# An ELU's tail written as a product, with the PSUM readers put first

## The chip, the cores and the metric

One core of one Trainium2 chip runs the kernel. The metric is the device time of one execution in microseconds (us). Engines by their names in the profile: PE (matmul), PEld (weight load), DVE (vector), ACT (activation), POOL (GpSimd), SP (which issues most of the transfers). Each engine works off its own instructions strictly in order and waits on signals of the others.

## The reference, cut to what matters

Three layers follow each other: a linear attention, a mixture of four ReLU experts, and one wide layer with an ELU between two matrix products. The change lies in the last one:

```
h = x @ w_in                      # x: 2304 x 512, w_in: 512 x 2048
g = where(h > 0, h, exp(min(h, 0)) - 1)
out = g @ w_out                   # w_out: 2048 x 512
```

## The kernel before

The products are made in fp32 quality: each operand is split into a high and a low part, and each product is three matmuls (high by high, high by low, low by high). The ELU layer runs as 12 steps, numbered i = 18 to 29: 4 slices of the hidden width (`s` = 6 to 9) by 3 blocks of tokens (`b`). A step has two halves (`fp` = 0, 1), and a half makes a 2 by 2 block of quarters of h by Strassen's scheme with 7 products, p = 0 to 6, each six matmuls on a 128x384 PSUM bank (L1165).

Four PSUM banks A, B, C, D (tiles `h` and `m`, two of each) turn round: the halves exchange A with C and B with D. In a half, p0 goes to C and p1 to B; p2 adds to B, and DVE makes D from it (L1454); p3 adds to A, which is then quarter A11; p4 adds to B, and DVE makes C from it (L1465, called the C add below), which is quarter A22; p5 adds to D, quarter A21; p6 adds to B, quarter A12. The next half's p1 overwrites the bank of A21 and its p0 that of A11, so a bank must have been read by then.

Each quarter goes through `elu` (96 calls: 12 steps, 2 halves, 4 quarters). Its three ACT steps are issued at once; its DVE steps are put into the list `pend` and issued by `run_pend` behind the next product's work. The ACT order and the DVE order are thus fixed by where the code calls these functions; nothing is rescheduled. The names that rows show: `extra` and one `half` are the two buffers of the variable m, another `half` holds t, and the result g goes to `gt` or `half`. From step 21 on (`fast`), quarters are combined on DVE: S1, S2, S3 behind A21 (L1219 to L1221), S4 behind A12 (L1225). What results is split by `parts`: ACT copies the high part (L1187), POOL subtracts for the low part (L1188).

Between the products stand, by a table of places, the second layer's products of the step before (`turned_product`, L1294, 12 matmuls each), whose two PSUM banks are added into SBUF by DVE (L1303), and pieces of weight preparation for later steps (DVE L763, L768, L769, L774, L775, L809, ACT L752, L800, POOL L801). In steps 18 and 19 the next layer's input is also transposed and stored (ACT L957, L974, DVE L985, POOL L991). 

Of the kernel before, what the change touches and what calls it, by code (L numbers as in the profile page):

```python
# [14 lines left out]
AF = mybir.ActivationFunctionType  # L15
ALU = mybir.AluOpType
# [5 lines left out]
def tile_attention_moe_moe(  # L22
# [13 lines left out]
    nc = tc.nc  # L36
# [490 lines left out]
    def bank(which):  # L527
        pool = ps_h if which == "h" else ps[which]
        return pool.tile([P, ps.get((which, "wide"), 1), 512], F32, tag=which, name=which)
# [5 lines left out]
    t = bank("o")  # L535
# [64 lines left out]
    for i in range(NP_):  # L600
        late = i >= NPAIR
        t = K_START[i - NPAIR] if late else HALF_STEP * i
# [243 lines left out]
    for b in range(NB):  # L846
        need = min(NP_, -(-2 * TB * (b + 1) // S) * NPAIR)
        t = 66 + 36 * b
# [302 lines left out]
    def fast(i):  # L1151
        return 0 <= i < len(STEPS) and SEVEN[STEPS[i][0]]

    def turned(i):
        return 0 <= i < len(STEPS) and STEPS[i][0] >= S_MOE

    def product(i, fp, p, dst):
        s, b = STEPS[i]
        wname, xname, o = PRODUCTS[p]
        t, c = w1s[s, fp][wname]  # L1160
        x = [y.rearrange("p (d n) -> p d n", d=2) for y in ring(len(OPS) * i + p)]
        n = 0
        for dl in range(2):
            for wl, xl_ in ((0, 0), (0, 1), (1, 0)):
                nc.tensor.matmul(  # L1165
                    dst, t[:, wl, c + dl, :], x[xl_][:, dl, :], start=(n == 0 and p < 2), stop=(n == 5),
                    skip_group_check=True,
                )
                n += 1
# [5 lines left out]
            out=gl, in0=h, scalar=0.0, in1=gh.bitcast(F32), op0=ALU.max, op1=ALU.subtract  # L1175
        )

    waiting, pend = [], []
    halves, turns = {}, [0]

    def flush():
# [3 lines left out]
    def parts(key, g):  # L1185
        gh, gl = take(*key)
        nc.scalar.activation(out=gh, in_=g, func=AF.Copy)  # L1187
        nc.gpsimd.tensor_tensor(out=gl, in0=g, in1=gh.bitcast(F32), op=ALU.subtract)  # L1188

    def run_pend():  # L1190
        while pend:
            pend.pop(0)()

    def elu(i, h, fp, name):

        if not halves:
            for tag, n in (("qh", 2), ("ql", 2), ("y", 1)):
                t = tmp.tile([P, n * TB], F32, tag=tag, name="half")
                halves[tag] = [t[:, k * TB : (k + 1) * TB] for k in range(n)]
        n = turns[0] % 2  # L1200
        turns[0] += 1
        m, t = (e_, halves["y"][0])[n], halves["qh"][n]
        nc.scalar.activation(out=m, in_=h, func=AF.Relu, scale=-1.0)
        nc.scalar.activation(out=t, in_=m, func=AF.Tanh, scale=-0.5)
        nc.scalar.activation(out=m, in_=m, func=AF.Exp, scale=-1.0)
        if fast(i) and "s4" not in halves:
            halves["s4"] = tmp.tile([P, TB], F32, tag="ek", name="s4")
        g11, g22, s1, s2 = (gt[:, k] for k in range(4))
        g21, g12 = halves["ql"]
        tt = nc.vector.tensor_tensor  # L1210
        g = dict(A11=g11, A22=g22, A21=g21, A12=g12)[name] if fast(i) else halves["ql"][n]

        def rest():
            nc.vector.scalar_tensor_tensor(out=m, in0=m, scalar=1.0, in1=t, op0=ALU.add, op1=ALU.mult)  # L1214
            nc.vector.scalar_tensor_tensor(out=g, in0=h, scalar=0.0, in1=m, op0=ALU.max, op1=ALU.add)  # L1215
            if not fast(i):
                todo = [((int(name[1]) - 1, 2 * fp + int(name[2]) - 1), g)]
            elif name == "A21":
                tt(out=s1, in0=g21, in1=g22, op=ALU.add)  # L1219
                tt(out=s2, in0=s1, in1=g11, op=ALU.subtract)  # L1220
                tt(out=g21, in0=g21, in1=g11, op=ALU.subtract)  # L1221
                todo = [(("S1", fp), s1), (("S2", fp), s2), (("S3", fp), g21)]
            elif name == "A12":
                s4 = halves["s4"]
                tt(out=s4, in0=g12, in1=s2, op=ALU.subtract)  # L1225
                todo = [(("S4", fp), s4), (("A12", fp), g12)]
            else:
                todo = [((name, fp), g)]
            for key, x in todo:
                waiting.append(lambda key=key, x=x: parts((i, *key), x))  # L1230

        pend.append(rest)

    def chunk(i, c):
# [190 lines left out]
    for i, (s, b) in enumerate(STEPS):  # L1425
        moe, fill = s < S_MOE, {}
        if fast(i - 1):
            one, places = (turned_product, TURNED_PLACES) if turned(i - 1) else (second_product, PLACES)
            fill = {n: (one, i - 1, k) for k, n in enumerate(places)}
        elif turned(i - 1):  # L1430
            fill = {n: (group, i - 1, *g) for g, n in zip(GROUPS, GROUP_PLACES)}
        elif i > 0:
            fill = {n: (chunk, i - 1, c) for c, n in zip(CHUNKS, (1, 3, 5, 8, 10, 12) if moe else (1, 2, 5, 8, 9, 12))}
        hooks = TURNED_HOOKS if turned(i - 1) else MIXED if fast(i - 1) else PLAIN if moe else EARLY
        if i + 1 == len(STEPS):
            hooks = {}
        for fp in range(2):
            A_, B_, C_, D_ = (A, B, C, D) if fp == 0 else (C, D, A, B)
            banks = {"A": A_, "B": B_, "C": C_, "D": D_}
            f1, f2 = 2 * fp, 2 * fp + 1  # L1440
            for p in range(len(PRODUCTS)):
                idx = 7 * fp + p
                goal[0] = i * SH + hooks[idx] if idx in hooks else hook2_n[0]
                product(i, fp, p, banks[PRODUCTS[p][2]])
                seven = fast(i)
                if p == 0:
                    nc.scalar.activation(out=s5, in_=C_, func=AF.Copy)
                    run_pend()
                elif p == 1:
                    nc.scalar.activation(out=A_, in_=B_, func=AF.Copy)  # L1450
                    flush_late()
                    flush()
                elif p == 2:
                    nc.vector.tensor_tensor(out=D_, in0=B_, in1=s5, op=ALU.add)  # L1454
                elif p == 3:
                    if moe and seven:
                        quarter_a11(i, fp, A_)
                    elif moe:
                        relu(i, A_, f1, 0)
                    else:  # L1460
                        elu(i, A_, fp, "A11")
                        if idx in fill:
                            run_pend()
                elif p == 4:
                    nc.vector.tensor_tensor(out=C_, in0=B_, in1=s5, op=ALU.add)  # L1465
                    if moe and seven:
                        direct(i, "A22", fp, C_)
                    elif not moe:
                        run_pend()
                        elu(i, C_, fp, "A22")  # L1470
                        flush()
                elif p == 5:
                    if moe and seven:
                        late.extend(quarter_a21(i, fp, D_))
                    elif not moe:
                        run_pend()
                        elu(i, D_, fp, "A21")
                        flush()
                elif p == 6:
                    if idx in fill and moe and fast(i - 1):  # L1480
                        fn, *args = fill.pop(idx)
                        fn(*args)
                    if seven and moe:
                        last = quarter_a12(i, fp, B_)
                        flush_late()
                        late.append(last)
                    elif moe:
                        relu(i, B_, f2, 0)
                    else:
                        run_pend()  # L1490
                        elu(i, B_, fp, "A12")
                        if not seven:
                            flush()
                drain()
                flush_adds()
                if fp == 1:
                    if p == 0:
                        ring_load(len(OPS) * (i + 1))
                    if p < 6:
                        ring_load(len(OPS) * (i + 1) + p + 1)  # L1500
                for _ in range({1: 2, 3: 1, 5: 1, 8: 2, 10: 2}.get(idx, 0) if i == 0 else 0):
                    pieces.pop(0)()
                if idx in fill:
                    fn, *args = fill.pop(idx)
                    fn(*args)
                tick(True)
                if p == 5 and moe and not seven:
                    relu(i, D_, f1, 1)
                    relu(i, C_, f2, 1)
# [59 lines left out]
```

## Time and profile before

| what | value |
|---|---|
| median of 3 runs | 1201.7 us (1200.88 to 1202.17) |
| span of the profiled execution | 1201.4 us |
| granted TensorE clock, mean | 0.994 |
| busy over the span: PE, DVE, ACT, POOL | 97%, 75%, 56%, 53% |
| the ELU layer, from about 808 us to the end | 394 us |

The profiled execution's own time is its span; the median of the runs is 0.3 us above it. PE's busy time is modelled from the starts of pipelined matmuls, so its stalls are read from the idle time ahead of single matmuls, and DVE's and ACT's idle times from theirs. The stretch that counts is the ELU layer, and in it the places where PE stands still.

### The profile page before, as it was taken

How to read it: one execution, taken by the hardware profiler on the slowest of the kernel's cores; microseconds unless marked ns; L12 is line 12 of the kernel's file. 1: busy time of each engine (PE TensorE's matmuls, PEld its weight loads, DVE VectorE, ACT ScalarE, POOL GpSimd, SP SyncE). 2: the span in 40 equal slices, each digit the busy share in tenths (PEclk: the TensorE clock that was granted, in tenths of full speed). 3: DMA queues.
4: the chain of work that ended last, by engine and by line, in shares of the span. 5: the costliest groups of instructions: out<-in, count | busy, mean ns of one | idle time of the engine just before them, and what ended most of it. 6: DMA issues, size and time to landing. Idle time of an engine off the chain costs nothing.

```text
span 1201.4 us, 21064 instructions
## 1 busy us (share of the span) xinstructions
PE 1170.6 (97%) x7516; PEld 1115.4 (93%) x7516; DVE 903.5 (75%) x1525; ACT 673.7 (56%) x1430; POOL 636.7 (53%) x602
## 2 busy tenths in 40 slices
PE   7799999999999999999999999999999999999998
PEld 6688889889999999999999999998999999899898
DVE  6977887655787787787787786566566879879875
ACT  6544544335455455455455453357777777777763
POOL 4622543017468468468468463356535756756744
PEclk7999999999999999999999999999999999999999
DMA  9444666766666666766767767998985465465362
GB/s 254 125 128 154 209 223 212 251 225 220 249 233 245 252 231 245 254 229 246 254 229 245 255 228 264 318 346 268 328 303 203 170 223 176 175 235 184 139 236 105
DMA packets 157399, 272.34 MB, mean 227 GB/s; under 512 B 12784, under 2 KB 83952, under 8 KB 157296
## 3 DMA queue, kind: packets, MB, share of 16 engines
q1 hardware_dynamic: 155568, 267.87, 64.8%
q10 hardware_dynamic: 1728, 3.15, 0.7%
q8 instruction: 59, 0.97, 0.3%
q14 instruction: 44, 0.36, 0.1%
HBM read 224.83 MB, written 46.14 MB: 226 GB/s over the span
## 4 chain that ended last, share of the span: by engine, by line
PE 75%; DVE 12%; ACT 5%; DMA 3%; issue 3%; POOL 2%; SPq 0%; DVEq 0%; POOLq 0%; ACTq 0%
PE o L1383 19%; PE h L1165 14%; PE m L1165 14%; PE h L1021 7%; PE o L1021 7%; PE o L1294 5%; DVE accs L1303 1%; PE o L1249 1%; PE o L1248 1%; PE o L1247 1%; PE o L1269 1%; PE o L1268 1%; PE o L1267 1%; DVE half L1215 1%; DVE extra L1214 1%
## 5 line engine op out<-in xcount | busy, mean ns | idle before, releaser
L1165 PE MATMUL m<-xh,w1s 128*128 128x384 f32 x840 | 246.5, 338 | 5.9 <-DVE half L1215 3.2
L1165 PE MATMUL h<-xh,w1s 128*128 128x384 f32 x840 | 244.9, 337 | 2.6 <-ACT m L1450 1.5
L1165 PEld LDWEIGHTS m<-xh,w1s 128*128 128x128 f32 x840 | 154.2, 188 | 12.0 <-DVE half L1215 4.1
L1165 PEld LDWEIGHTS h<-xh,w1s 128*128 128x128 f32 x840 | 154.8, 188 | 6.1 <-ACT m L1450 2.6
L1165 PE MATMUL m<-xl,w1s 128*128 128x384 f32 x420 | 140.7, 335 | 0.2 <-DMA xl<-xs 0.2
L1165 PE MATMUL h<-xl,w1s 128*128 128x384 f32 x420 | 140.8, 335 | 0.0
L1021 PE MATMUL o<-w2t,hpa 128*128 128x512 f32 x432 | 118.0, 400 | 0.8 <-DVE hpa L1053 0.5
L1021 PE MATMUL h<-xh,w1t 128*128 128x256 f32 (+1 forms) x512 | 112.4, 298 | 0.1
L1021 PEld LDWEIGHTS h<-xh,w1t 128*128 128x128 f32 x512 | 86.4, 193 | 5.2 <-POOL w1t L442 0.3
L1383 PE MATMUL o<-w2g,xh 128*128 128x256 f32 x540 | 90.4, 282 | 0.0
L801 POOL TENSOR_TENSOR w2g<-r,w2g 128x512 fp32r<-128x512 f32 x56 | 77.1, 1385 | 24.0 <-ACT w2g L800 20.2
L1021 PEld LDWEIGHTS o<-w2t,hpa 128*128 128x128 f32 x432 | 75.5, 189 | 14.9 <-DVE hpa L1053 2.4
L1383 PE MATMUL o<-w2g,hpa 128*128 128x256 f32 x540 | 89.0, 282 | 0.0
L1383 PE MATMUL o<-w2g,xl 128*128 128x256 f32 x540 | 87.3, 282 | 0.0
L1405 DVE SCALAR_TENSOR_TENSOR accs<-o,pn,accs 128x256 f32<-128x256 f32 x180 | 75.7, 476 | 14.8 <-PE o L1383 14.2
L1165 PEld LDWEIGHTS m<-xl,w1s 128*128 128x128 f32 x420 | 78.9, 188 | 1.1 <-DMA xl<-xs 0.5
L1165 PEld LDWEIGHTS h<-xl,w1s 128*128 128x128 f32 x420 | 79.2, 189 | 0.3
L1383 PEld LDWEIGHTS o<-w2g,xh 128*128 128x128 f32 x540 | 78.0, 190 | 0.1
L1021 PE MATMUL h<-xl,w1t 128*128 128x256 f32 (+1 forms) x256 | 77.6, 303 | 0.0
L1383 PEld LDWEIGHTS o<-w2g,hpa 128*128 128x128 f32 x540 | 76.1, 190 | 0.2
L1383 PEld LDWEIGHTS o<-w2g,xl 128*128 128x128 f32 x540 | 75.6, 190 | 0.2
L1303 DVE TENSOR_TENSOR accs<-o,accs 128x768 f32<-128x768 f32 (+1 forms) x64 | 59.7, 936 | 11.1 <-PE o L1294 11.1
(314 smaller groups left out, 2987.3 us busy)
## 6 DMA issues: line engine op xcount, KB each, us to landing
xh<-xs SPq DMA_DIRECT2D x210, 384.0 KB, 5.6
xl<-xs SPq DMA_DIRECT2D x210, 384.0 KB, 6.2
r<-in_w_dram SPq DMA_DIRECT2D x56, 256.0 KB, 4.4
xs<-xh SPq DMA_DIRECT2D x21, 384.0 KB, 3.9
xs<-xl SPq DMA_DIRECT2D x21, 384.0 KB, 4.1
xs<-stage SPq DMA_DIRECT2D x29, 256.0 KB, 5.0
r<-scratch SPq DMA_DIRECT2D x24, 256.0 KB, 3.8
xs<-gt SPq DMA_DIRECT2D x21, 256.0 KB, 4.5
```

Of the source, the lines that this page charges most:

```text
L801: nc.gpsimd.tensor_tensor(out=t[:, 1], in0=src, in1=t[:, 0].bitcast(F32), op=ALU.subtract)
L1021: nc.tensor.matmul(out, lhsT, rhs, **kw)
L1165: nc.tensor.matmul(dst, t[:, wl, c + dl, :], x[xl_][:, dl, :], start=(n == 0 and p < 2), stop=(n == 5), skip_group_check=True,)
L1214: nc.vector.scalar_tensor_tensor(out=m, in0=m, scalar=1.0, in1=t, op0=ALU.add, op1=ALU.mult)
L1215: nc.vector.scalar_tensor_tensor(out=g, in0=h, scalar=0.0, in1=m, op0=ALU.max, op1=ALU.add)
L1247: nc.tensor.matmul(o, gh, w[:, 0, :], start=(f == 0), stop=False)
L1248: nc.tensor.matmul(o, gh, w[:, 1, :], start=False, stop=False)
L1249: nc.tensor.matmul(o, gl, w[:, 0, :], start=False, stop=(f == FS - 1))
L1294: nc.tensor.matmul(y[:, m], l, r, start=(n == 0 and k in STARTS), stop=(n == 5), skip_group_check=True)
L1303: nc.vector.tensor_tensor(out=a, in0=y[:, ms], in1=a, op=ALU.add)
L1383: nc.tensor.matmul(o, l, r, start=(first_write and m == 0 and c != 1), stop=(m == 5), skip_group_check=True)
L1405: nc.vector.scalar_tensor_tensor(out=a, in0=sums[x][:, c * HALF_M : (c + 1) * HALF_M], scalar=pr, in1=a, op0=ALU.mult, op1=ALU.add)
```

## The change

Before, an ELU is max(h, 0) + (1 + exp(-m)) * tanh(-m/2), with m = max(-h, 0). ACT makes m from PSUM, then Tanh and Exp of m from SBUF; DVE makes the product in SBUF, and last reads h from PSUM again for the maximum and the sum. After, it is (1 + exp(-m)) * max(h/2, tanh(h/2)). ACT makes Tanh of h/2 from PSUM, then m from PSUM, then Exp from SBUF; DVE makes the maximum from PSUM (`begin`), and last the product from SBUF alone. The numbers of instructions on every engine stay the same: three on ACT and two on DVE for each quarter. `begin` goes to a list of its own, `begun`. It is issued in front of the C add for quarter A11, and in `run_pend` just ahead of the product for the others.

```
-    waiting, pend = [], []
+    waiting, pend, begun = [], [], []
...
+    def run_begun():
+        while begun:
+            begun.pop(0)()
+
     def run_pend():
+        run_begun()
         while pend:
             pend.pop(0)()
...
+        nc.scalar.activation(out=t, in_=h, func=AF.Tanh, scale=0.5)
         nc.scalar.activation(out=m, in_=h, func=AF.Relu, scale=-1.0)
-        nc.scalar.activation(out=t, in_=m, func=AF.Tanh, scale=-0.5)
         nc.scalar.activation(out=m, in_=m, func=AF.Exp, scale=-1.0)
...
+        def begin():
+            nc.vector.scalar_tensor_tensor(out=t, in0=h, scalar=0.5, in1=t, op0=ALU.mult, op1=ALU.max)
+
         def rest():
-            nc.vector.scalar_tensor_tensor(out=m, in0=m, scalar=1.0, in1=t, op0=ALU.add, op1=ALU.mult)
-            nc.vector.scalar_tensor_tensor(out=g, in0=h, scalar=0.0, in1=m, op0=ALU.max, op1=ALU.add)
+            nc.vector.scalar_tensor_tensor(out=g, in0=m, scalar=1.0, in1=t, op0=ALU.add, op1=ALU.mult)
...
+        begun.append(begin)
         pend.append(rest)
...
                 elif p == 4:
+                    run_begun()
                     nc.vector.tensor_tensor(out=C_, in0=B_, in1=s5, op=ALU.add)
```

DVE in the first half of step 23, quarters A11, A22 and A21, before (L1465 is the C add, L1214 the product, L1215 the maximum and sum that reads PSUM, L1303 the second layer's addition):

```order
L1465 TENSOR_TENSOR m<-m,extra 128x384
L1214 SCALAR_TENSOR_TENSOR extra<-extra,half 128x384
L1215 SCALAR_TENSOR_TENSOR gt<-h,extra 128x384
L1214 SCALAR_TENSOR_TENSOR half<-half 128x384
L1215 SCALAR_TENSOR_TENSOR gt<-m,half 128x384
L1303 TENSOR_TENSOR accs<-o,accs 128x768
L1214 SCALAR_TENSOR_TENSOR extra<-extra,half 128x384
L1215 SCALAR_TENSOR_TENSOR half<-h,extra 128x384
```

The same place in the changed kernel (L1219 is `begin`, L1474 the C add, L1222 the product, L1311 the addition):

```order
L1219 SCALAR_TENSOR_TENSOR half<-h,half 128x384
L1474 TENSOR_TENSOR m<-m,extra 128x384
L1222 SCALAR_TENSOR_TENSOR gt<-extra,half 128x384
L1219 SCALAR_TENSOR_TENSOR half<-m,half 128x384
L1222 SCALAR_TENSOR_TENSOR gt<-half 128x384
L1311 TENSOR_TENSOR accs<-o,accs 128x768
L1219 SCALAR_TENSOR_TENSOR half<-h,half 128x384
L1222 SCALAR_TENSOR_TENSOR half<-extra,half 128x384
```

For A11 the PSUM reader has moved in front of the C add; for A22 and A21 the two steps have changed places, PSUM reader first, and nothing else has moved.

ACT in the same place, A11, A22, two copies and A21, before (L1203 Relu, L1204 Tanh, L1205 Exp):

```order
L1203 ACTIVATE extra<-h 128x384
L1204 ACTIVATE half<-extra 128x384
L1205 ACTIVATE extra<-extra 128x384
L1203 ACTIVATE half<-m 128x384
L1204 ACTIVATE half<-half 128x384
L1205 ACTIVATE half<-half 128x384
L1187 ACTIVATE hpa<-gt 128x384
L752 ACTIVATE w1s<-r 128x512
L1203 ACTIVATE extra<-h 128x384
```

And in the changed kernel (L1208 Tanh, L1209 Relu, L1210 Exp):

```order
L1208 ACTIVATE half<-h 128x384
L1209 ACTIVATE extra<-h 128x384
L1210 ACTIVATE extra<-extra 128x384
L1208 ACTIVATE half<-m 128x384
L1209 ACTIVATE half<-m 128x384
L1210 ACTIVATE half<-half 128x384
L1187 ACTIVATE hpa<-gt 128x384
L752 ACTIVATE w1s<-r 128x512
L1208 ACTIVATE half<-h 128x384
```

Tanh and Relu both read the PSUM bank and no longer depend on each other; Exp still follows Relu. In the built program, 94 of the 96 Tanh raise no signal of their own: the Relu behind each raises the count for both, so whoever waits for the Tanh waits until the Relu has ended.

## Rows read from the trace of the kernel before

**Rows 1.** Timeline of PE, stalls: start, us, instruction, idle before and its releaser.

```profile
936.02 0.44 PE L1165 MATMUL m<-xh,w1s 128*128 128x384 f32 x1 [0.75 <-DVE half L1215]
...
987.12 0.44 PE L1165 MATMUL h<-xh,w1s 128*128 128x384 f32 x1 [0.27 <-DVE m L1454]
...
1004.82 0.45 PE L1165 MATMUL m<-xh,w1s 128*128 128x384 f32 x1 [1.12 <-DVE h L1454]
...
1034.08 1.15 PE L1294 MATMUL o<-hpa,w2g 128*128 128x384 f32 x5 [0.95 <-DVE accs L1303]
```

**Rows 2.** Group of line L1204 (Tanh) on ACT: busy us, mean ns, idle before.

```profile
L1204 ACT ACTIVATE half<-half 128x384 f32<-128x384 f32 x48 | 25.3, 527 | 1.5
```

**Rows 3.** Lines L1214, L1215 and L809's waits on DVE: ns least, median, most.

```profile
L1214 DVE SCALAR_TENSOR_TENSOR half<-half x48: 544/557/1651, 817.1 to 1183.6; 128x384 f32<-128x384 f32 x48
L1215 DVE SCALAR_TENSOR_TENSOR half<-h,extra x15: 557/558/560, 815.9 to 1166.5; 128x384 f32<-128x384 f32 x15
L809 DVEq EVENT_SEMAPHORE  x22: 21/49/50, 267.7 to 1115.3; - x22
```

**Rows 4.** Timeline near 507 us, expert layer: two ACT readers of a bank, one DVE.

```profile
506.97 0.49 ACT L1332 ACTIVATE xl<-m 128x384 fp32r<-128x384 f32 x1 [0.77 <-DVE m L1465]
507.36 0.49 ACT L1334 ACTIVATE gt<-m 128x384 f32<-128x384 f32 x1
507.94 0.56 DVE L1335 SCALAR_TENSOR_TENSOR xl<-m,xl 128x384 fp32r<-128x384 f32 x1 [1.01 <-ACT gt L1334]
```

**Rows 5.** Timeline of ACT, step 23, quarters A11, A22 (Relu and Exp), A21.

```profile
973.36 0.49 ACT L1203 ACTIVATE extra<-h 128x384 f32<-128x384 f32 x1 [3.68 <-PE h L1165]
...
975.00 0.49 ACT L1203 ACTIVATE half<-m 128x384 f32<-128x384 f32 x1
...
976.09 0.53 ACT L1205 ACTIVATE half<-half 128x384 f32<-128x384 f32 x1
...
977.52 0.49 ACT L1203 ACTIVATE extra<-h 128x384 f32<-128x384 f32 x1
```

**Rows 6.** Timeline of DVE, step 23, first half: C add, A22, A21.

```profile
974.40 0.57 DVE L1465 TENSOR_TENSOR m<-m,extra 128x384 f32<-128x384 f32 x1 [1.12 <-PE m L1165]
...
976.64 0.56 DVE L1214 SCALAR_TENSOR_TENSOR half<-half 128x384 f32<-128x384 f32 x1 [0.42 <-ACT half L1205]
...
979.16 0.56 DVE L1214 SCALAR_TENSOR_TENSOR extra<-extra,half 128x384 f32<-128x384 f32 x1 [0.43 <-ACT extra L1205]
```

**Rows 7.** Timeline of DVE, 988 to 1012 us, where it is nearly always busy.

```profile
988.49 0.57 DVE L1465 TENSOR_TENSOR h<-h,extra 128x384 f32<-128x384 f32 x1 [0.56 <-PE h L1165]
...
990.73 0.94 DVE L1214 SCALAR_TENSOR_TENSOR half<-half 128x384 f32<-128x384 f32 x1 [0.23 <-ACT half L1205]
...
1007.66 0.55 DVE L1214 SCALAR_TENSOR_TENSOR extra<-extra,half 128x384 f32<-128x384 f32 x1
1008.32 0.56 DVE L1215 SCALAR_TENSOR_TENSOR gt<-h,extra 128x384 f32<-128x384 f32 x1
1008.79 0.68 DVE L763 TENSOR_TENSOR w1s<-r,w1s 128x512 fp32r<-128x512 f32 x1
...
1011.85 0.72 DVE L1214 SCALAR_TENSOR_TENSOR extra<-extra,half 128x384 f32<-128x384 f32 x1 [0.34 <-ACT extra L1205]
```

**Rows 8.** Timeline of DVE, step 21, quarter A21.

```profile
933.96 1.34 DVE L1214 SCALAR_TENSOR_TENSOR extra<-extra,half 128x384 f32<-128x384 f32 x1 [1.79 <-ACT extra L1205]
```

**Rows 9.** The chain that ended last, 847 to 1197 us: start, us, what.

```profile
854.04 0.43 ACT xh L1187
...
859.97 1.34 PE h L1165 x6
...
863.39 1.04 PE m L1165 x6
...
1180.50 0.57 DVE half L1215
...
1186.34 10.71 PE o L1294 x60
```

## The prediction

> **What bounds the kernel now.** I read first the chain that ended last, then the timeline of PE for the places where it stands still, then the timelines of DVE and ACT ahead of each such place. PE is busy nearly everywhere, so only what shortens a stall of PE can shorten the run. In the ELU layer PE has about 14 stalls worth seeing; the reader finds four of them in [rows 1]. They have different owners: 936.02 waits for L1215, the ELU's last step, which holds a PSUM bank; 987.12 and 1004.82 wait for DVE's additions of products; 1034.08 waits for the second layer's addition. A stall costs more than its idle time: six matmuls take 1.34 us behind one and 1.04 us in flow [rows 9], so each costs its idle time and 0.3 us.
>
> Then the question is what the releaser waited for. In the two stretches with weight preparation, 973 to 1034 us and the same pattern again from 1067 to 1127 us, DVE runs almost without a gap and PE waits for it. There DVE's few idle moments are on the path, and they are waits for the ELU's Exp: 0.42, 0.43, 0.23 and 0.34 us [rows 6, 7]. A bank that is freed sooner is worth nothing by itself there: PE would go on and stand longer at the next addition, as at 1034.08. In steps 18, 19 and 21 the path runs through ACT's ELU steps, and the last 10.71 us of PE start when the last ELUs are done [rows 9].
>
> **The change for one quarter.** Call S the start of its first ACT step. Before, for A22 of step 23: S is 975.00, Exp ends at 976.09 + 0.53 = S + 1.62 [rows 5], L1214 starts at S + 1.64 [rows 6], L1215 follows 0.66 us behind it [rows 7] and takes 0.56 us [rows 3]. So g is done, and the bank free, at S + 2.86.
>
> After, the two PSUM readers do not wait for each other. The nearest rows are the pair of Relus on one bank in the expert layer: the second starts 0.39 us after the first, ends at S + 0.88, and the DVE reader of the bank starts only behind the second, at S + 0.97 in the row shown [rows 4], though it needs the first alone. That is the same folding of signals that the built program has for Tanh and Relu, so I take S + 0.94 for `begin`, not S + 0.51. The time of a Tanh from PSUM no row shows; it lies between 0.49 us, a Relu from PSUM [rows 5], and 0.53 us, a Tanh from SBUF [rows 2]; I take 0.49, since in the rows what is read, not the function, sets it. Exp then runs from S + 0.90 to S + 1.43, 0.19 us sooner. `begin` ends at S + 1.50 and frees the bank, 1.36 us sooner; the product starts at about S + 1.60 and g is done at S + 2.16: 0.7 us sooner wherever DVE was waiting for Exp. Where DVE comes late anyway, g gains nothing: two steps of the same length as before.
>
> DVE has as many steps as before, one reading PSUM and one SBUF alone. The PSUM one always takes 0.56 us; the SBUF one takes between 0.54 and 1.65 us, by what POOL does meanwhile [rows 3]. It now comes second instead of first. I count that at zero, for the same number of steps meets the same POOL work; one step that changes sides is worth 0.8 us either way (1.34 in [rows 8] against 0.56), and that goes into the range.
>
> **What is moved.** For A11 `begin` stands in front of the C add. That add ran at S + 1.04 in step 23 (973.36 to 974.40, [rows 5, 6]). `begin` starts at S + 0.94 and the next independent step 0.47 us later [rows 7], so the add slips to S + 1.4, 0.35 us late, and behind it on DVE and ACT the ELU of A22. The add is that tight in 17 of the 24 half-steps. This is the price of the change; in flow it is covered by the 0.7 us that A22's own chain gains, and PE needs that bank only products later.
>
> An ordering gain: between a step and one that needs its result lie 0.66 us from start to start, between independent ones 0.47 [rows 7]. For A11 the C add now stands between the two ELU steps, which saves 0.15 to 0.2 us a quarter, 0.3 us in each weight stretch (two such quarters where DVE is saturated). Against it, most products now wait for one signal more; a queue wait takes 0.02 us for one signal and 0.05 for two [rows 3], some 0.2 us in a stretch. Net 0.1. The Trainium skill, "VectorE: DVE Perf Modes", section "The DRAIN you can't avoid", says that a semaphore between two DVE steps costs nothing extra, as the pipe empties in any case. By that the net term would be zero and the time 0.2 us longer; the rows contradict it here.
>
> **The sum, against the profiled execution.**
> Steps 18 and 19: ACT's A22 and A21 lie on the path to POOL and to the stalls (854.04 to 859.97, [rows 9]); two ELUs of 0.19 us less. A22's start does not slip here, as ACT had a copy to do first. 0.35 us, twice: 0.7 (0 if the slip counts).
> Step 21: ACT reaches A21 0.2 us sooner. DVE waited 1.79 us, then took 1.34 [rows 8]; before, g was done at 933.96 + 1.34 + 0.1 + 0.56 = 935.96. After, `begin` is done while Exp runs, and the product follows: near 935.05. 0.9 us, under the 0.75 + 0.3 that PE loses there.
> First weight stretch: A22 of step 23 starts 0.35 late and ends 0.35 early; A21 starts as before (PE sets it) and ends 0.7 early, so DVE is 0.7 ahead and the stall at 987.12 (0.27 + 0.3) goes. At 988.49 the C add waited for PE [rows 7]; with `begin` ahead of it, 0.2 of that is kept. A22 gains 0.7 again: 0.9. From there DVE has no gap until 1011.85, where 0.34 us of waiting goes: 1.25. With the ordering net 1.35 us, and it reaches 1034.08. The second stretch is the same: 2.7 together.
> The end: A21 of the last half waits for Exp, and the path leads from its L1215 at 1180.50 by additions to 1186.34 [rows 9]: 0.7.
> Sum 0.7 + 0.9 + 2.7 + 0.7 = 5.0. Span 1201.4 - 5.0 = 1196.4; the median of the runs lay 0.3 above the span, so **1196.7 us**.
>
> Bounds: at the low end 1.0 for steps 18 and 19, 1.05, 2.0 in each stretch, 0.9 at the end and one contended step fewer (0.8), 7.8 in all: 1193.9. At the high end 0, 0.3, 0.3 each and 0.3 with one contended step more, 0.4 in all: about 1201.
>
> **The rivals.**
> DVE's sum decides in the weight stretches: if what it waits less is only waited elsewhere (for PE, or behind the later C add), the 2.7 us go and 1199.4 remains; with half of the other terms gone too, 1200.5. For it: DVE is saturated there, and work, not waiting, fills it. Against it: the waits of [rows 6, 7] are followed by DVE steps without a gap up to the stall. Chance 0.18, no change.
> The product, now last, is the contended step (slower): in the two weight stretches there are 24 of these SBUF steps, and half of them took about 0.56 us. Each that comes to lie beside a POOL step costs 0.8. Six eat the gain, nine give 1201.7 - 5.0 + 7.2 = 1203.9. For it: POOL's work follows the ELU's results, so a sooner `begin` moves the product relative to it. Against it: as many can move out as in. Chance 0.08.
> More than forecast: the stalls at the bank of A21, as 936.02, were thought to move on to the next addition; if DVE's contended steps also fall away, the low end and below, 1193.5. Chance 0.1.
> That the change does not free the bank sooner, because of the folded signal, is counted already: S + 1.5, not S + 1.1.
>
> **How the numbers follow.** The forecast has 0.64 (1194 to 1199.2), the larger gain 0.1, no change 0.18, slower 0.08. About 0.2%, 2.4 us, is what a measurement of this kernel can tell from no change. Faster 0.74, same 0.18, slower 0.08. The range from 1193.9 to 1200.9 leaves out about 0.05 below and 0.12 above.
>
> **What would show it.** Right: on ACT the second PSUM step 0.39 us behind the Tanh and Exp's end at S + 1.43; on DVE `begin` starting at the Relu's end; no PE wait for the ELU's DVE steps; the C add 0.35 us later in the half-steps that flow; the stall near 1034 at about the same length, but 4 us sooner in the run. Wrong: a `begin` at the Tanh's end (the gain is larger), PE waits for the C add or for ACT's copies, or SBUF products that mostly take 0.8 us and more where L1214's median was 0.56 [rows 3], which would be the slower rival.

## The result, and the profile after

The changed kernel takes 1215.15 us (median; 1212.99 to 1216.53) against 1201.7 us before (1199.13 to 1204.45): a ratio of 1.0112, 95% interval 1.0099 to 1.0124. It is 13.4 us slower where 5.0 us of gain were forecast, and it lies outside the range. The profiled execution has a span of 1214.7 us, 13.3 us above that of before. A run's time is some 1.8 us above its own span (here 1216.53 us); the 0.3 us named further up lay between one run's span and the median of others, and cancels in the differences.

The stalls of PE come first, as in [rows 1]. These are the four largest of PE's waits in the changed kernel from 905 us to the end (two more are 0.3 us each; L1462 is the addition into D, L1458 ACT's copy of a product into a bank, L1311 the second layer's addition; columns: who <- for whom, us in total, times, longest):

```profile
PE h L1165 <- DVE m L1462: 8.1, 7, 1.3
PE o L1302 <- DVE accs L1311: 5.1, 6, 1.2
PE m L1165 <- ACT h L1458: 4.2, 3, 1.7
PE m L1165 <- DVE h L1462: 2.2, 2, 1.1
```

Two lines of the same view of the kernel before:

```profile
PE m L1165 <- DVE half L1215: 3.2, 3, 1.2
...
PE h L1165 <- DVE m L1454: 0.6, 2, 0.3
```

No matmul waits for the ELU's DVE steps any more; before, such waits made 3.2 us, of which 936.02 in [rows 1] is one. In their place stands the wait for the addition into D, 0.6 us before with m as its bank and 8.1 us now. So DVE comes later, though it has the same instructions. The lines of the ELU's DVE steps tell where its time went. For the changed kernel (L1222 is the product, one of its four tile forms, L1226 is S1, L1232 S4; ns least, median, most):

```profile
L1222 DVE SCALAR_TENSOR_TENSOR half<-half x30: 557/559/1041, 816.8 to 1196.7; 128x384 f32<-128x384 f32 x30
L1226 DVE TENSOR_TENSOR gt<-half,gt x18: 1249/1256/1261, 917.6 to 1192.9; 128x384 f32<-128x384 f32 x18
L1232 DVE TENSOR_TENSOR s<-half,gt x18: 557/1250/1533, 921.7 to 1197.5; 128x384 f32<-128x384 f32 x18
```

And the same S1 and S4 in the kernel before (L1219, L1225):

```profile
L1219 DVE TENSOR_TENSOR gt<-half,gt x18: 570/632/670, 919.1 to 1181.1; 128x384 f32<-128x384 f32 x18
L1225 DVE TENSOR_TENSOR s<-half,gt x18: 557/630/1361, 922.6 to 1184.8; 128x384 f32<-128x384 f32 x18
```

The product, which the forecast watched, did not change: its median is that of L1214 in [rows 3], and all 96 of them take 64.8 us against 65.6 us before. The two steps *behind* it doubled. S1 took 0.63 us and takes 1.25 us, in all 18 instances and within 12 ns; S4 went from 0.63 to 1.25 us in the median. Summed over its steps, DVE works 335.0 us from 808 us on instead of 315.6. S1 and S4 are 18.6 us of these 19.4, S2 has 3.4 us more, and all the rest together 2.6 us less.

Why S1 takes double is seen when POOL's timeline is laid beside DVE's. Quarter A21 of step 24 in the changed kernel, DVE first (columns: start, us, engine, line, operation), from the product to the addition into D, and the matmul that waits for it:

```profile
1014.11 0.89 DVE L1222 SCALAR_TENSOR_TENSOR half<-extra,half 128x384 f32<-128x384 f32 x1
1015.03 1.25 DVE L1226 TENSOR_TENSOR gt<-half,gt 128x384 f32<-128x384 f32 x1
...
1018.55 0.69 DVE L1222 SCALAR_TENSOR_TENSOR half<-half 128x384 f32<-128x384 f32 x1
1019.28 1.25 DVE L1232 TENSOR_TENSOR s<-half,gt 128x384 f32<-128x384 f32 x1
...
1021.32 0.55 DVE L1462 TENSOR_TENSOR m<-h,extra 128x384 f32<-128x384 f32 x1
```

```profile
1014.54 1.33 POOL L1188 TENSOR_TENSOR xh<-gt,xh 128x384 fp32r<-128x384 f32 x1
...
1018.79 1.32 POOL L1188 TENSOR_TENSOR xh<-gt,xh 128x384 fp32r<-128x384 f32 x1
```

```profile
1021.93 0.44 PE L1165 MATMUL h<-xh,w1s 128*128 128x384 f32 x1 [1.29 <-DVE m L1462]
```

POOL's subtraction starts while the product runs, at 1014.54, and ends at 1015.87. S1 begins at 1015.03 and ends at 1016.28, 0.41 us behind POOL's end. S4 does the same: POOL ends at 1020.11, S4 at 1020.53. In all 18 cases a subtraction of POOL starts 0.27 to 0.50 us ahead of S1 and ends 0.83 to 0.85 us behind S1's start. Its end thus follows the product's by 0.87 us, however early it started on record: it had waited for the product, and S1 then waits for it. The same place in the kernel before, DVE and POOL, whose product is in [rows 7] at 1011.85:

```profile
1012.68 0.56 DVE L1215 SCALAR_TENSOR_TENSOR half<-h,extra 128x384 f32<-128x384 f32 x1
1013.27 0.59 DVE L1219 TENSOR_TENSOR gt<-half,gt 128x384 f32<-128x384 f32 x1
...
1016.70 0.60 DVE L1225 TENSOR_TENSOR s<-half,gt 128x384 f32<-128x384 f32 x1
...
1018.08 0.55 DVE L1454 TENSOR_TENSOR m<-h,extra 128x384 f32<-128x384 f32 x1
```

```profile
1012.31 1.14 POOL L1188 TENSOR_TENSOR xh<-gt,xh 128x384 fp32r<-128x384 f32 x1 [0.15 <-ACT xh L1187]
```

There, too, POOL's subtraction starts under the product. But the step behind the product was L1215, which reads one operand from PSUM; it ran its usual 0.56 us beside POOL, and when S1 came POOL had 0.18 us left. The reading to be tested: a DVE step with both operands in SBUF and a POOL operation exclude each other, and a POOL operation that waits beside one such step goes ahead of the next one. The change put the PSUM reader ahead of the product, so that three steps with both operands in SBUF now stand in a row, and S1 pays. The Trainium skill, "SBUF — State Buffer", section "Who interferes with whom", says that a VectorE instruction with two SBUF inputs contends with a GpSimd instruction that reads SBUF, and that the one that starts second blocks until the first is done. These rows agree (S1 1.25 us beside it, L1215 0.56 us). That the one waiting gets its turn between two VectorE steps in a row the rows show and that section doesn't say.

From the start of A21's product to the start of the addition into D there were 6.23 us before (1011.85 to 1018.08) and are 7.21 us now (1014.11 to 1021.32), though one step of about 0.6 us, the PSUM reader, has moved out of the stretch. Step by step S1 has 0.66 us more, S4 0.65 us and the two products 0.31 us.

How the loss grows over the run is seen from ACT's copy of product p0 (L1447 before, L1455 after), one for each half. The table holds its start against the kernel before, in us, set to zero at the layer's first such copy (step 18, 803.9 us before). The other columns are kernels of the experiments below; the last line is the span.

| half (time before) | after | PSUM last (e1) | mixed (e6) | A12 last (e9) | A21 last (e10) | before, short POOL (e5) | after, short POOL (e4) |
|---|---|---|---|---|---|---|---|
| 18, second (825.7) | -0.2 | -0.3 | -0.2 | -0.3 | -0.2 | -0.7 | -1.0 |
| 21, first (905.5) | -0.5 | -1.2 | -0.4 | -0.8 | -0.7 | -1.5 | -1.9 |
| 22, first (936.1) | -0.9 | -1.4 | -0.8 | -1.1 | -1.0 | -1.4 | -2.3 |
| 22, second (952.5) | -0.2 | -1.0 | -0.3 | -0.7 | -0.3 | -2.2 | -3.0 |
| 23, second (981.7) | 1.0 | -1.1 | -0.2 | -0.6 | 0.9 | -2.2 | -3.0 |
| 25, first (1027.6) | 3.6 | -1.4 | -0.2 | 0.7 | 3.6 | -4.6 | -6.1 |
| 26, second (1075.0) | 6.8 | -1.2 | -0.2 | 2.5 | 6.4 | -5.5 | -6.8 |
| 28, first (1120.9) | 9.4 | -1.5 | 0.2 | 3.8 | 9.1 | -7.9 | -9.9 |
| 29, second (1168.8) | 12.8 | -1.1 | 0.1 | 6.9 | 11.9 | -9.2 | -11.2 |
| end (1201.4) | 13.6 | -1.3 | 0.2 | 6.8 | 12.6 | -9.1 | -11.8 |

Up to the start of step 22 the changed kernel is ahead. S1 to S4 exist from step 21 on, and from step 22 on it loses 1.9 us a step, with weight preparation or without.

### The profile page after: what moved, and what is told of

Read it like the earlier page. It is cut to its first block, busy times and chain, and to the rows that moved or that the text cites. A ratio compares the mean times of both kernels' runs of the same rounds, so it can differ in the third digit from the quotient of the medians.

```text
span 1214.7 us, 21071 instructions
## 1 busy us (share of the span) xinstructions
PE 1174.3 (97%) x7516; PEld 1119.2 (92%) x7516; DVE 917.1 (75%) x1525; ACT 660.0 (54%) x1430; POOL 640.2 (53%) x602
## 4 chain that ended last, share of the span: by engine, by line
PE 75%; DVE 12%; ACT 5%; issue 3%; DMA 2%; POOL 2%; DVEq 0%; SPq 0%; ACTq 0%; POOLq 0%
PE o L1391 19%; PE h L1165 14%; PE m L1165 14%; PE h L1021 7%; PE o L1021 6%; PE o L1302 5%; DVE accs L1311 2%; DVE half L1222 1%; PE o L1256 1%; PE o L1257 1%; PE o L1255 1%; PE o L1277 1%; PE o L1275 1%; PE o L1276 1%; DVE half L1219 1%
## 5 line engine op out<-in xcount | busy, mean ns | idle before, releaser
L1311 DVE TENSOR_TENSOR accs<-o,accs 128x768 f32<-128x768 f32 (+1 forms) x64 | 59.7, 935 | 14.3 <-PE o L1302 14.3
```

The source lines that it names most:

```text
L1311: nc.vector.tensor_tensor(out=a, in0=y[:, ms], in1=a, op=ALU.add)
```

## The experiments

The theory (T1) is the reading above. The rivals: the addition into C, or what stands ahead of it, is late (T2); two PSUM readers on ACT with one signal cost the time (T3); S1 is slow because it reads at once what the step ahead wrote (T4); it is the number of SBUF-only steps, wherever they stand (T5). Each ratio is against runs of the kernel before made along with that experiment (medians of 1200.7 to 1201.8 us), so a difference of 1 or 2 us between two experiments is uncertain.

**e1: the new order on ACT, the old order on DVE.** The product in SBUF first, the maximum from PSUM last; no `begin`.

```
-            nc.vector.scalar_tensor_tensor(out=g, in0=m, scalar=1.0, in1=t, op0=ALU.add, op1=ALU.mult)
+            nc.vector.scalar_tensor_tensor(out=m, in0=m, scalar=1.0, in1=t, op0=ALU.add, op1=ALU.mult)
+            nc.vector.scalar_tensor_tensor(out=g, in0=h, scalar=1.0, in1=m, op0=ALU.mult, op1=ALU.max)
...
-        begun.append(begin)
```

> ACT as in the changed kernel (Tanh and Relu from PSUM), but DVE in the order of before: the product in SBUF first, then g = max(h, product), which reads PSUM, last. No step stands in front of the C add. Theory T1 (the port that DVE and POOL share: the product in SBUF alone now stands right in front of S1 and S4, which also read SBUF alone; POOL's subtraction gets in between and S1 waits for all of it): S1 falls from 1.26 us back to about 0.63, S4 from 1.14 to about 0.75, and the time to that of before or a little below, 1198 to 1202. Rival T2 (the step in front of the C add holds the path up): also back to about 1201. Rival T3 (two PSUM readers on ACT, and the folded signal, cost the time): stays near 1215.

1199.89 us, ratio 0.9989 (0.9980 to 0.9998). S1:

```profile
L1227 DVE TENSOR_TENSOR gt<-half,gt x18: 570/626/939, 915.5 to 1177.5; 128x384 f32<-128x384 f32 x18
```

The whole loss sits in DVE's order; ACT's new order alone loses nothing. T3 falls. It is also the fastest of the kernels that do all the work, but by 0.1% only, which is less than the 0.2% that count as a difference here.

**e2: the old order on ACT, the new one on DVE.**

```
-        nc.scalar.activation(out=t, in_=h, func=AF.Tanh, scale=0.5)
         nc.scalar.activation(out=m, in_=h, func=AF.Relu, scale=-1.0)
+        nc.scalar.activation(out=t, in_=m, func=AF.Tanh, scale=-0.5)
```

> DVE as in the changed kernel, ACT in the order of before (Relu from PSUM, Tanh and Exp from SBUF). T1: S1 stays at 1.26 us in all 18 places, and the time near 1215, a few us above for the slower ACT steps. T2: slow too, since the step stands in front of the C add and waits longer. T3: back to about 1201.

1223.54 us, ratio 1.0193 (1.0179 to 1.0207). S1 is as slow as in the changed kernel (1.26 us in the mean), and the first line of PE's waits is worse:

```profile
PE h L1165 <- DVE m L1462: 13.3, 7, 3.2
```

That is more than the few us expected. With DVE's order as it is, ACT's new order is worth 8.4 us by the medians and 9.7 us by the ratios: it hides part of the loss and is not its cause.

**e3: no `begin` ahead of the C add.** The line `run_begun()` there is taken out, so that for A11, too, the maximum stands just ahead of the product.

> The changed kernel with the one call in front of the C add taken out, so that A11's PSUM step stands behind the C add. T1: S1 stays at 1.26 us and the time within 3 us of 1215. T2: the time falls to about 1202 or below. T3: stays near 1215, as by T1; the first kernel of this set tells those two apart.

1214.72 us, ratio 1.0112 (1.0097 to 1.0127): the changed kernel's time. S1 1.21 us, S4 1.14 us in the mean. T2 falls.

**e6: PSUM reader last for A21 and A12 alone,** the quarters behind which S1 and S4 stand; A11 and A22 as changed.

```
+            if name in ("A21", "A12"):
+                nc.vector.scalar_tensor_tensor(out=m, in0=m, scalar=1.0, in1=t, op0=ALU.add, op1=ALU.mult)
+                nc.vector.scalar_tensor_tensor(out=g, in0=h, scalar=1.0, in1=m, op0=ALU.mult, op1=ALU.max)
+            else:
...
+        if name in ("A11", "A22"):
+            begun.append(begin)
```

> The changed kernel for quarters A11 and A22; for A21 and A12, behind which S1 and S4 stand, the product first and the PSUM reader last. T1: S1 near 0.63 us and S4 near 0.75, and the gain that was forecast comes out in part: 1196 to 1200. T2: the call in front of the C add is still there, so the time stays near 1213. T3: stays near 1215.

1203.93 us, ratio 1.0019 (1.0010 to 1.0028). S1 and S4 are quick again (0.65 and 0.79 us in the mean) and 11.2 us of the 13.4 come back, but the gain I expected from A11's and A22's early banks does not show. S2 now meets POOL in 7 of 18 cases, and sums to 16.8 us instead of 12.0 before. DVE, then POOL:

```profile
949.97 0.59 DVE L1230 TENSOR_TENSOR gt<-half,gt 128x384 f32<-128x384 f32 x1
950.59 1.69 DVE L1231 TENSOR_TENSOR gt<-gt 128x384 f32<-128x384 f32 x1
```

```profile
950.57 1.30 POOL L801 TENSOR_TENSOR w2g<-r,w2g 128x512 fp32r<-128x512 f32 x1 [0.43 <-ACT w2g L800]
```

Here POOL's operation, one of the weight preparation, starts 0.02 us ahead of S2, and S2 ends 0.41 us behind its end.

**e4 and e5: POOL's subtraction cut to a quarter,** in the changed kernel (e4) and in the one before (e5). This takes the suspected cause away and leaves DVE's code as it is.

```
-        nc.gpsimd.tensor_tensor(out=gl, in0=g, in1=gh.bitcast(F32), op=ALU.subtract)
+        n = TB // 4
+        nc.gpsimd.tensor_tensor(out=gl[:, :n], in0=g[:, :n], in1=gh[:, :n].bitcast(F32), op=ALU.subtract)
```

> The changed kernel with POOL's low-part subtraction of the ELU layer cut to 96 of its 384 columns; it leaves three quarters of those low parts unmade, and nothing else is touched. Theory (DVE's steps that read SBUF alone wait for a POOL operation under way): POOL's operation of about 1.3 us shrinks to well under half, so S1 (18 times 1.25 us in the changed kernel, sum 22.6 us) falls to a median of at most 0.75 us, and S4 (sum 20.6 us) to at most 0.75 us; DVE's busy time in the layer falls from 332 us to 318 us or less; the time falls from 1215.2 us to 1194-1202 us, that is, to the kernel before with the same cut or up to 5 us under it. Rival (S1 is slow because it reads at once what the step ahead of it wrote): S1 stays at 1.25 us, whatever POOL does, and the time stays 10 us or more above the kernel before with the same cut.

> The kernel before with the same cut of POOL's subtraction (96 of 384 columns; three quarters of the low parts are left unmade). It is what the changed kernel with that cut is to be held against. Theory: there POOL's operations are hidden for the most part, so little is won: 1195-1201 us, S1 at about 0.6 us, the matmul waits on the D add stay. Rival (S1 slow by reading what was just written): the same here, 1197-1202 us; the two differ by their gap to the changed kernel, 0 to 5 us in its favour by the theory, over 10 us against it by the rival.

e4: 1189.48 us (1189.28 to 1190.86), ratio 0.9905 (0.9891 to 0.9920). e5: 1193.84 us (1192.58 to 1194.09), ratio 0.9936 (0.9919 to 0.9952). S1 and S4 in e4, and all that PE still waits for from 905 us on:

```profile
L1227 DVE TENSOR_TENSOR gt<-half,gt x18: 559/632/636, 916.0 to 1168.8; 128x384 f32<-128x384 f32 x18
```

```profile
L1233 DVE TENSOR_TENSOR s<-half,gt x18: 557/558/1535, 919.5 to 1172.5; 128x384 f32<-128x384 f32 x18
```

```profile
PE o L1303 <- DVE accs L1312: 2.6, 3, 1.2
```

And one of the two S1 of e4 that have no POOL operation beside them:

```profile
1020.94 0.56 DVE L1227 TENSOR_TENSOR gt<-half,gt 128x384 f32<-128x384 f32 x1
```

This decides it. S1 stands just as close behind the product (0.03 us) and reads what the product wrote, yet it takes 0.63 us, and 0.56 us where no POOL operation is beside it: T4 falls. In the other 16 instances S1 still ends 0.41 to 0.42 us behind the end of POOL's now shorter operation. DVE has the same SBUF-only steps in the same order. And with POOL's operation short the change is a gain of 4.4 us by the medians (3.2 us by the spans, 2.7 us by the table), against the 5.0 us that the forecast had worked out for it. So nothing of the loss is left without POOL's full subtraction. That 4.4 us comes so near the forecast's sum is in part luck: the cut takes most of PE's other stalls away in both kernels, and each weight stretch gave 0.7 us instead of the 1.35 forecast. Both kernels were faster than expected: the kernel before, too, gains 0.64% by the cut, 7.7 us.

**e8: the mixed kernel (e6) with the same cut.**

> The mixed kernel (maximum first for A11 and A22, PSUM reader last for A21 and A12) with the same cut of POOL's subtraction (96 of 384 columns, the rest of the low parts left unmade). It ran 1.0019 of the kernel before with POOL whole. Theory: what it lost was S2 behind POOL (sum 16.8 us against 12.0 us), so with a short POOL operation S2 is back at 0.6-0.7 us and the earlier release of A11's and A22's banks shows: 1 to 4 us under the kernel before with the same cut. Rival (the early release is worth nothing, because the addition into D or a second-layer addition is late next): within 1 us of the kernel before with the same cut, with S2 quick.

1192.12 us (1191.69 to 1192.58), ratio 0.9925 (0.9910 to 0.9940): 1.7 us under e5, as the theory said, and 2.6 us above e4, with S2 at 0.56 us. But e8 differs from e5 by ACT's new order as well, which alone put e1 1.3 us ahead in the table. What the early banks alone are worth is not shown.

**e7: the second layer's addition between A21's product and S1.** It reads PSUM; it stood ahead of A21's maximum. The operations and their number are the changed kernel's.

```
             elif name == "A21":
+                flush_adds()
                 tt(out=s1, in0=g21, in1=g22, op=ALU.add)
...
-                flush_adds()
+                if moe or not seven or p != 5:
+                    flush_adds()
```

> The changed kernel with one thing moved: the second layer's addition (which reads PSUM, 0.95 us) that stands ahead of quarter A21's maximum stands between A21's product and S1. Same operations and numbers. Theory: the POOL operation that slips in at the product's end now runs under a step that reads PSUM, so S1 falls from 1.25 us to 0.55-0.75 us in at least 12 of its 18 instances (the sum from 22.6 to 11-15 us); S4, whose place is unchanged, stays near 20 us. The time falls by part of that: 1204-1212 us, since the addition comes some 1.2 us later and may hold the next second-layer matmuls. Rival (the changed kernel loses through the number of its steps that read SBUF alone, wherever they stand): S1 stays over 1 us, or its loss appears in the steps next to it, and the time stays 1213-1217 us.

1214.53 us, ratio 1.0110 (1.0095 to 1.0126). DVE in the place of step 23, and S1's line:

```profile
978.73 0.56 DVE L1222 SCALAR_TENSOR_TENSOR half<-extra,half 128x384 f32<-128x384 f32 x1
979.21 0.95 DVE L1312 TENSOR_TENSOR accs<-o,accs 128x768 f32<-128x768 f32 x1
980.08 0.55 DVE L1227 TENSOR_TENSOR gt<-half,gt 128x384 f32<-128x384 f32 x1
```

```profile
L1227 DVE TENSOR_TENSOR gt<-half,gt x18: 541/548/1257, 916.4 to 1191.4; 128x384 f32<-128x384 f32 x18
```

For S1 the mechanism is confirmed: one PSUM reader in between and S1 takes 0.55 us in the median, with POOL's work and the number of steps unchanged. The two at 1.26 us are those of step 21, where no addition stands in between. T5 falls for S1's duration, and DVE works 11.4 us less, although S2 has 1.2 us more. My time was wrong: nothing is won. In the changed kernel the addition ran while DVE would have waited for A21's activations (with it gone, DVE idles 0.97 us ahead of A21's maximum in step 24); now it lies in the stretch up to the addition into D, and puts in 0.87 us (979.21 to 980.08) where S1 gives back 0.7. The wait for the addition into D stays at 8.2 us.

**e9 and e10: PSUM reader last for A12 alone (e9), for A21 alone (e10).** The edit is e6's with one name in place of two.

> The changed kernel with quarter A12 alone in the old DVE order (product in SBUF, PSUM reader last, just ahead of S4). Theory (the loss is the time of S1 and S4 in the stretch of DVE work from A21's maximum to the addition into D, 0.65 us each in a half): S4 falls from 1.14 us to 0.65-0.85 us on average, S1 stays at 1.25 us; the addition into D comes some 0.65 us sooner in a half, the matmul waits on it (8.1 us, seven times, in the changed kernel) about halve, and the time is about half way back: 1206-1210 us. Rival (the loss comes from the PSUM readers of ACT or from the number of steps that read SBUF alone): 1213-1217 us, the waits on the addition into D unchanged.

> The changed kernel with quarter A21 alone in the old DVE order (PSUM reader last, just ahead of S1). Theory: S1 falls from 1.25 us to 0.6-0.75 us, S4 stays near 1.14 us; S2 may take up part of it (it did in the mixed kernel, 0.93 us on average); the rest shows as in the kernel with A12 alone: 1206-1211 us. Unlike the kernel that put an addition between the product and S1, this one puts no other work into the stretch, so S1's gain must show in the time. Rival: S1 is quick again and the time stays 1213-1217 us, as it did there.

e9: 1207.89 us, ratio 1.0046 (1.0029 to 1.0064), inside the range expected; S4 0.74 us in the mean, S1 still 1.29. The waits on the addition into D are down from 8.1 us to this:

```profile
PE h L1165 <- DVE m L1467: 3.1, 4, 1.3
```

e10: 1213.65 us, ratio 1.0099 (1.0084 to 1.0115). S1 is quick (0.65 us), but only 1.5 us are won, less than the two intervals can tell apart; I expected four or more. In it, DVE near 1029 us:

```profile
1029.41 0.86 DVE L1230 TENSOR_TENSOR gt<-half,gt 128x384 f32<-128x384 f32 x1
1030.31 1.25 DVE L1231 TENSOR_TENSOR gt<-gt 128x384 f32<-128x384 f32 x1
```

```profile
1029.82 1.32 POOL L1188 TENSOR_TENSOR xh<-gt,xh 128x384 fp32r<-128x384 f32 x1
```

POOL's operation comes a little later against DVE here and squeezes in between S1 and S2, so S2 pays. Besides, A21's DVE work can now begin only behind Exp and no more behind Relu, half a microsecond later. So half of the loss hangs on A12's order (S4, the last obstacle ahead of the addition into D); A21's is worth 1.5 us alone, by the medians, and 3 to 4 us once S4 is quick (from e9 to e6, 4.0 by the medians, 3.2 by the ratios). From e6 to e1, A11's and A22's order, come another 4.0 us by the medians (1.5 us by the spans in the table; the profiled run of e6 lay 1.9 us under its median). S2 does not explain that: it has 6.7 us more in e6 than in e1, but S3 has 3.3 us less, and DVE's steps sum to 1.3 us less in all; and 0.8 us arise by the start of step 21 already, ahead of any S2. This part stays open.

**e11 and e12: S2, S3 and S4 moved behind the next half's addition into D,** in the changed kernel (e11) and in the one before (e12), their splits behind A11's activations. The aim was a faster kernel than both.

```
...
                 elif p == 2:
                     nc.vector.tensor_tensor(out=D_, in0=B_, in1=s5, op=ALU.add)
+                    run_late()
...
                         elu(i, A_, fp, "A11")
+                        flush()
```

> The changed kernel with S2, S3 and S4 issued behind the next half's addition into D, and not ahead of it (their splits follow quarter A11's activations); all work is kept. Theory: the stretch from A21's maximum to the addition into D loses S2, S3 and S4, 0.56-0.86 + 0.55 + 1.14 us, more than the 1.3 us that matmuls wait there, so these waits (8.1 us) go; S4 now stands behind S3 and may be slow or not, and it costs nothing there unless quarter A11's product is late. Time 1196-1204 us. Rival (the loss is not the stretch ahead of the addition into D): 1212-1217 us, or the wait turns up at A11's or A22's bank and the time is 1204-1212 us.

> The kernel before with the same move of S2, S3 and S4 behind the next half's addition into D. Theory: the waits on the addition into D (2.8 us) and on quarter A21's reading (3.2 us) in the kernel before shrink, as DVE reaches them 1.7 us sooner: 1194-1199 us. Rival (these waits are bound by other work, or A11's quarter is now late, since S2 to S4 stand ahead of its product): 1199-1204 us.

e11: 1212.40 us, ratio 1.0087 (1.0072 to 1.0102). e12: 1222.38 us, ratio 1.0170 (1.0155 to 1.0186). In e11 the waits on the addition into D do fall, as the theory says, to the second line here; the first and others like it take their place:

```profile
PE o L1311 <- POOL xh L1188: 1.7, 3, 0.8
...
PE h L1165 <- DVE m L1471: 0.4, 2, 0.2
```

The split results now reach POOL too late for the second layer's matmuls. In e12 PE waits 9.7 us, eight times, for A21's PSUM reader: the splits of S2 to S4 stand on ACT ahead of A22's and A21's activations. Both expectations failed in the time. DVE's stretch was freed and the work moved into ACT's and POOL's.

## Why the prediction was wrong, step by step

**One quarter: right to 0.04 us.** A22 of step 23 in the changed kernel, ACT, then DVE:

```profile
976.10 0.49 ACT L1208 ACTIVATE half<-m 128x384 f32<-128x384 f32 x1 [0.54 <-DVE m L1474]
976.49 0.48 ACT L1209 ACTIVATE half<-m 128x384 f32<-128x384 f32 x1
977.01 0.53 ACT L1210 ACTIVATE half<-half 128x384 f32<-128x384 f32 x1
```

```profile
975.51 0.56 DVE L1474 TENSOR_TENSOR m<-m,extra 128x384 f32<-128x384 f32 x1
...
977.01 0.56 DVE L1219 SCALAR_TENSOR_TENSOR half<-m,half 128x384 f32<-128x384 f32 x1 [0.48 <-ACT half L1209]
977.70 0.56 DVE L1222 SCALAR_TENSOR_TENSOR gt<-half 128x384 f32<-128x384 f32 x1
```

The second PSUM step follows 0.39 us behind the first, Exp ends at S + 1.44 (forecast 1.43), `begin` starts at S + 0.91, at the Relu's end as the folded signal says (0.94), the product at S + 1.60 (1.60), and g is done at S + 2.16 (2.16). The C add stands at 975.51 with A11's S at 974.13: S + 1.38 (1.4). Independent DVE steps lie 0.47 us apart, dependent ones 0.69.

One count was off: the C add stands 1.04 to 1.07 us behind A11's S in 18 of the 24 half-steps, not in 17.

**Steps 18 and 19: right in sign.** By the mark of the table the changed kernel is 1.2 us ahead when step 20 begins (874.0), for a forecast of 0.7; when step 21 begins 0.5 of that is left.

**Step 21: the wait at A21's bank went, and another came.** The matmul of 936.02 [rows 1] does not wait any more; the first one of the product behind it does, 0.85 us for ACT's copy L1458. Of the 0.9 us forecast, 0.4 came by the start of step 22. The chain is seen more plainly at its sister in step 24:

```profile
1031.31 1.25 DVE L1226 TENSOR_TENSOR gt<-half,gt 128x384 f32<-128x384 f32 x1
...
1033.54 0.68 DVE L809 TENSOR_TENSOR r<-r 128x512 f32<-128x512 f32 x1
```

```profile
1034.26 0.63 ACT L800 ACTIVATE w2g<-r 128x512 fp32r<-128x512 f32 x1 [2.85 <-DVE r L809]
1034.80 0.47 ACT L1458 ACTIVATE h<-m 128x384 f32<-128x384 f32 x1
```

```profile
1035.32 0.44 PE L1165 MATMUL m<-xh,w1s 128*128 128x384 f32 x1 [1.67 <-ACT h L1458]
```

ACT's copy is ready to go, but stands behind a piece of weight preparation that waits 2.85 us for DVE's L809, and L809 stands behind the slow S1. "PE waits for ACT's copies" was named as a sign of being wrong; I had not followed ACT's queue to DVE.

**The weight stretches: wrong in sign.** The forecast took 1.35 us off each. From 981.7 to 1027.6 us (time before), and again from 1075.0 to 1120.9, the changed kernel loses 2.6 us. With POOL short, e4 wins 3.1 us in each and e5 2.4: the change gives 0.7 us there, right in sign and half the size. And the steps between them, on which the forecast had no term at all, lose 3.2 us (1027.6 to 1075.0) and 3.3 us (1120.9 to 1168.8); S1 and S4 stand in every step from 21 on. With POOL short, e4 loses only 0.2 us against e5 in the first of them and nothing in the second.

**The end: wrong by S1 and S4.** The forecast had 0.7 us of gain from A21's activations to the last second-layer products. The chain that ended last, in the changed kernel:

```profile
1192.32 0.57 DVE half L1222
1192.91 1.27 DVE gt L1226
...
1196.70 0.81 DVE half L1222
1197.53 1.25 DVE s L1232
...
1199.70 10.69 PE o L1302 x60
```

From A21's first activation to that last row it was 8.14 us (1178.20 to 1186.34, [rows 9]) and is 8.98 us (1190.72 to 1199.70): S1 0.62 us, S4 0.66 and the last product 0.33 more. In e4 against e5 the end wins about 0.7 us (2.7 us ahead at the span's end, 2.0 us at 1168.8), the forecast's very number.

**The step that failed** is the sentence on the SBUF product: "It now comes second instead of first. I count that at zero, for the same number of steps meets the same POOL work." The number is right and the product's own sum is (64.8 us for 65.6). What was never priced is the *neighbour*. Before, each product had a PSUM reader behind it, under which most of POOL's waiting operation ran (S1 0.63 us, for 0.56 with none beside it). After, A21's and A12's have S1 and S4 behind them. Of 36 such places 32 take 1.25 us or more: 29 of them 0.5 to 0.7 us more than before, the other three, slow before already, 0.17 to 0.19 more. They stand ahead of the addition into D, which PE then waits for. [rows 3, 8] could not show them, for they list only the ELU's two steps; S1's and S4's rows, 0.63 us in the median of before, showed steps that were sheltered. The price could be read all the same: three of the 18 S4 before took 1.35 us behind a POOL operation of the weight preparation, and two of the S2 1.54 us. The slower rival named the right two engines, but moved the price to the product and bounded it at 24 steps of the weight stretches, nine of them slow.

## What to carry to other kernels

Where VectorE and GpSimd share work, price an operation by its neighbours: a VectorE step that reads PSUM is a gap in which GpSimd's waiting operation runs almost free (S1 0.63 us behind it, 1.25 us without it), and taking it out of a row of SBUF-only steps moves GpSimd's whole operation onto the next of them. Before reordering, list for each such row what stands behind the moved step, and whether a GpSimd operation becomes ready there. A quicker step gives time back only where it is what the stretch waits for: by the medians S1 alone won 0.6 us (e7) and 1.5 us (e10), S4 alone 7 us (e9). And follow a delayed step through the queues behind it: here a copy on ACT paid for it two waits further on.

## What the runs showed of the hardware

- A VectorE step with both operands in SBUF that finds a GpSimd operation under way ends 0.41 to 0.42 us behind that operation's recorded end, for S1 in all 18 cases of the changed kernel, where it took 1.249 to 1.261 us, and in 16 of e4. S2 took 1.69 us in e6, where GpSimd's operation had just begun. A PSUM reader beside it kept its 0.56 us.
- GpSimd gets in between two such VectorE steps with a gap of 0.03 us between them, if its operation started on record under the first: so it went in all 202 such places of the ELU layer in the fourteen traces. Ahead of S1 in the changed kernel that operation shows 1.10 to 1.34 us, where the least are 1.00 us, and ends 0.87 us behind the first step's end.
- Cutting GpSimd's subtraction to a quarter made the kernel before 0.64% (0.48 to 0.81) faster, although GpSimd is busy only 53% of the span.
